# Hash attention and RWKV channel mix on one core: one PSUM pool, joined bucket bits, attention output turned by DMA, wanted times per pair

## Chip, core, metric

One core of a Trainium2 chip (trn2). The metric is the device time of one execution in microseconds (us), the median of several. The kernel before takes 258.7 us (258.31 to 258.94 in three runs; with a fourth, the median is 258.6).

Engine names: PE is the matmul engine and PEld its weight loads, DVE the vector engine, ACT the scalar engine, POOL the third elementwise engine, SP the engine that issues most DMAs.

## The reference, cut to what matters

Four batches of eight heads, 768 rows of 64 columns. Each row of q and k gets a bucket number from the signs of six projections; a query sees only keys of its own bucket. The eight heads of a batch, side by side, are x (768 x 512) of the channel mix.

```python
q_bits = (einsum('bhsd,dk->bhsk', q, proj) > 0)        # k_bits the same
mask   = q_bucket[..., :, None] == k_bucket[..., None, :]
scores = where(mask, q @ k.T / sqrt(64), -1e9)
attn   = exp(scores - max) / sum                       # then attn @ v
# x: the heads of a batch side by side; x_prev: x moved down by one row
xk = mu_k * x + (1 - mu_k) * x_prev                    # xr the same with mu_r
k  = maximum(xk @ w_k, 0)
out = sigmoid(xr @ w_r) * ((k * k) @ w_v)
```

## The kernel before

It works on 16 pairs of heads, four to a batch; the channel mix of a batch can run once its four pairs are done. The instruction order is made while the kernel is built: every operation is given to a small planner with a duration, an engine and a wanted time; the planner plays the whole kernel through and emits the operations in that order. The order is fixed on every engine. In the traces the instructions of PE, ACT and DVE, and the DMAs that SP issues, follow the order of the built program one for one; an engine whose next instruction has to wait stands still.

The planner also hands out PSUM. PSUM is the memory that matmuls write to. The kernel uses it as eight banks (512 columns of 32 bits in each of 128 partitions). Before, they are declared as two score tiles of two banks and four small tiles of one bank each:

```python
sc_t = [psum.tile([P, STEP], FP32, name=f"sc{i}", tag=f"sc{i}") for i in range(2)]   # STEP = 1024: two banks
sm_t = [psum.tile([P, 512], FP32, name=f"sm{i}", tag=f"sm{i}") for i in range(4)]    # one bank
plan = Plan({"sc": (2, 2), "sm": (4, 3)})
def sm(name):
    return sm_t[plan.slot[name]]
```

The softmax here doesn't subtract the row's maximum and nothing guards it: scores larger than these inputs give would overflow.

## Time and profile before

| | before |
|---|---|
| device time, median | 258.7 us |
| span of the profiled run | 256.8 us |
| PE / DVE / ACT / POOL busy | 239.3 / 195.1 / 185.5 / 57.9 us |
| ACT idle, waiting for scores | 28.3 us |
| first matmul of the first channel mix | us 63.4 |

The head of the page of the kernel before: the span, the busy time of each engine with its share and number of instructions, and PE's row of the 40 equal slices (a digit is tenths busy).

```profile
span 256.8 us, 6319 instructions
...
PE 239.3 (93%) x2519; PEld 143.5 (56%) x2519; DVE 195.1 (76%) x391; ACT 185.5 (72%) x242; POOL 57.9 (23%) x98
...
PE   6768898888999999999999989999999999999994
```

PE has holes only in the first quarter and is full after that.

The page's groups of one step of the mix, before. Columns: line, engine, operation, out<-in, count | busy us, mean ns of one | idle us of the engine just before, and what ended it.

```profile
L652 PE MATMUL sm<-xk,wk 128*128 128x384 bf16 x256 | 48.9, 326 | 0.2
...
L656 ACT ACTIVATE kr<-sm 128x384 bf16<-128x384 f32 x64 | 31.3, 498 | 9.5 <-PE sm L652 7.5
...
L659 DVE TENSOR_TENSOR k<-kr 128x384 bf16<-128x384 bf16 x64 | 23.8, 385 | 8.5 <-ACT kr L656 8.4
```

PE stood 0.2 us in all before these 256 matmuls.

At us 20, in the start, ACT stood 3.9 us for scores of pair 0 (ACT's timeline of the kernel before):

```profile
20.20 2.90 ACT L557 ACTIVATE pt<-sc 128x1024 bf16<-128x1024 f32 x3 [3.86 <-PE sc L553]
```

### The profile page before, as it was taken

The page shows a single profiled execution, that of the slowest core. Times are in us where ns is not written, and L with a number is a line of the kernel's source. Part 1 is how long each engine was busy: PE and PEld are TensorE (multiplying, and loading weights), DVE is VectorE, ACT ScalarE, POOL GpSimd, SP SyncE. Part 2 cuts the span into 40 slices and gives each one's busy share as a digit, 9 for nine tenths or more (in the row PEclk, how much of TensorE's full clock was granted, in tenths as well). Part 3 has the DMA queues.
Part 4 walks back from the last instruction along what each step waited for, and adds up shares of the span by engine and source line. Part 5 has one row for each costly group of instructions (what it writes and reads, how often), then busy time and mean ns, then how long its engine had stood idle before and what let it go on. Part 6 is the DMA issues. An engine that isn't in the chain of part 4 may idle for free.

```text
span 256.8 us, 6319 instructions
## 1 busy us (share of the span) xinstructions
PE 239.3 (93%) x2519; PEld 143.5 (56%) x2519; DVE 195.1 (76%) x391; ACT 185.5 (72%) x242; POOL 57.9 (23%) x98
## 2 busy tenths in 40 slices
PE   6768898888999999999999989999999999999994
PEld 2334564555666456656666655555666666555441
DVE  4999676777789997989998999898685753675322
ACT  3838888888994598878898967586798986147320
POOL 2491415056051330504041424040000000000000
PEclk9998999999999999999999999999999999999999
DMA  6968979799998479796978987888200011220132
GB/s 191 382 168 155 163 174 172 199 171 180 225 201 227 116 199 175 212 241 190 274 148 266 216 241 149 233 164 166 89 3 6 3 41 43 82 86 1 41 123 82
DMA packets 64565, 39.78 MB, mean 155 GB/s; under 512 B 46756, under 2 KB 60952, under 8 KB 64536
## 3 DMA queue, kind: packets, MB, share of 16 engines
q1 hardware_dynamic: 62248, 36.76, 58.4%
q0 software_dynamic: 2208, 2.62, 6.3%
q8 instruction: 19, 0.31, 0.5%
q14 instruction: 10, 0.08, 0.1%
q10 hardware_dynamic: 80, 0.00, 0.0%
HBM read 24.12 MB, written 6.29 MB: 118 GB/s over the span
## 4 chain that ended last, share of the span: by engine, by line
PE 63%; DMA 15%; DVE 10%; POOL 3%; SPq 3%; issue 2%; ACT 2%; POOLq 0%; DVEq 0%
PE sc L553 16%; PE sm L681 15%; PE sm L652 11%; PE sm L583 10%; DMA vn<-in_v_dram 8%; PE sm L671 7%; PE sm L443 4%; DMA qn<-in_q_dram 3%; DMA ak<-kh 2%; POOL vt L360 2%; DMA kn<-in_k_dram 2%; PE sm L609 2%; ACT pt L557 2%; SPq L334 1%; DVE xk L635 1%
## 5 line engine op out<-in xcount | busy, mean ns | idle before, releaser
L557 ACT ACTIVATE pt<-sc 128x1024 bf16<-128x1024 f32 x144 | 143.2, 1028 | 29.9 <-PE sc L553 28.3
L553 PE MATMUL sc<-aq,ak 128*128 128x512 f16 (+1 forms) x384 | 84.6, 329 | 4.5 <-ACT pt L557 4.5
L553 PEld LDWEIGHTS <-ak 128*128 128x128 f16 x384 | 33.6, 98 | 31.1 <-issue 12.2
L652 PE MATMUL sm<-xk,wk 128*128 128x384 bf16 x256 | 48.9, 326 | 0.2
L681 PE MATMUL sm<-wv,k 128*128 128x512 bf16 x192 | 47.8, 379 | 1.1 <-DVE ob L599 1.1
L583 PEld LDWEIGHTS <-pt 128*128 128x128 bf16 x1152 | 42.9, 97 | 9.0 <-issue 0.6
L583 PE MATMUL sm<-va,pt 128*128 128x65 bf16 x1152 | 44.6, 193 | 0.0
L656 ACT ACTIVATE kr<-sm 128x384 bf16<-128x384 f32 x64 | 31.3, 498 | 9.5 <-PE sm L652 7.5
L652 PEld LDWEIGHTS <-wk 128*128 128x128 bf16 x256 | 24.1, 98 | 15.2 <-issue 0.3
L360 POOL TENSOR_TENSOR vt<-vn 128x384 f32<-128x384 f32 x12 | 15.1, 1256 | 71.5 <-DMA vn<-in_v_dram 71.5
L659 DVE TENSOR_TENSOR k<-kr 128x384 bf16<-128x384 bf16 x64 | 23.8, 385 | 8.5 <-ACT kr L656 8.4
L674 ACT ACTIVATE rs<-sm 128x512 f32<-128x512 f32 x24 | 14.4, 599 | 22.1 <-PE sm L671 18.9
L681 PEld LDWEIGHTS <-k 128*128 128x128 bf16 x192 | 18.4, 98 | 19.5 <-issue 1.3
L688 DVE SCALAR_TENSOR_TENSOR os<-rs,sm 128x512 f32<-128x512 f32 x24 | 16.3, 684 | 16.5 <-PE sm L681 16.4
L671 PE MATMUL sm<-wr,xr 128*128 128x512 bf16 x96 | 24.6, 379 | 0.0
L619 POOL COPY xt<-xt 128x127 bf16<-128x127 bf16 x16 | 8.4, 525 | 69.1 <-DVE xt L615 64.4
L447 DVE TENSOR_SCALAR bx<-sm 128x384 uint16<-128x384 uint16 (+1 forms) x32 | 16.4, 549 | 3.3 <-PE sm L443 2.6
L599 DVE TENSOR_TENSOR ob<-sm,rc 128x384 bf16<-128x384 f32 x32 | 17.8, 556 | 0.9
L405 DVE SCALAR_TENSOR_TENSOR kh<-kn,kh 128x768 f16<-128x768 f32 x15 | 18.3, 1219 | 0.1
L635 DVE SCALAR_TENSOR_TENSOR xk<-df,muk,xt 128x768 bf16<-128x768 bf16 x16 | 16.7, 1046 | 0.3
L443 PE MATMUL sm<-ak,p 128*32 128x384 f16 x124 | 14.4, 335 | 2.3 <-DVE ak L422 1.3
L635 DVE SCALAR_TENSOR_TENSOR xr<-df,mur,xt 128x768 bf16<-128x768 bf16 x16 | 16.1, 1018 | 0.0
(76 smaller groups left out, 195.3 us busy)
## 6 DMA issues: line engine op xcount, KB each, us to landing
vn<-in_v_dram SPq DMA_DIRECT2D x16, 384.0 KB
out_dram<-os SPq DMA_DIRECT2D x24, 256.0 KB
qn<-in_q_dram SPq DMA_DIRECT2D x15, 384.0 KB
kn<-in_k_dram SPq DMA_DIRECT2D x15, 384.0 KB
wk<-in_moe_w_k_dram POOLq DMA_DIRECT2D x4, 256.0 KB, 5.3
wv<-in_moe_w_v_dram POOLq DMA_DIRECT2D x4, 256.0 KB, 8.7
wr<-in_moe_w_r_dram POOLq DMA_DIRECT2D x2, 256.0 KB, 5.4
aq<-bx SPq DMA_DIRECT2D x31, 9.0 KB
```

What stands on the lines that cost most here:

```text
L360: nc.gpsimd.tensor_tensor(out=vt[:, :, :, 0:E], in0=src[:, :, 0:3, 0:E], in1=src[:, :, 3:6, 0:E], op=ALU.add)
L405: nc.vector.scalar_tensor_tensor(out=nh[:, :, D:P], in0=nat.rearrange("p j (c d) -> p (j c) d", d=D), scalar=QS, in1=nh[:, :, 0:D], op0=AL ...
L443: nc.tensor.matmul(ps[32 * i : 32 * i + 32, 0:HALF], w_, a[:, i // 2, h * HALF : (h + 1) * HALF], start=st, stop=not st)
L553: nc.tensor.matmul(ps[:, lo - s * STEP : hi - s * STEP], side_a["k"][sa][:, j, jc * P : (jc + 1) * P], side_a["q"][sa][:, j, q0 : q0 + hi ...
L557: nc.scalar.activation(out=pt_t[sp][:, s * STEP : (s + 1) * STEP], in_=sc_t[plan.slot[nm]], func=AF.Exp, bias=EBIAS, scale=ESC)
L583: nc.tensor.matmul(oo[:, ic * 65 : ic * 65 + 65], pt_t[sp][:, o : o + P], va_t[sa][:, j, jc, 0 : D + 1], start=(not uc and ic == 0 and jc ...
L635: nc.vector.scalar_tensor_tensor(out=dst[smx], in0=df_t[sd], scalar=mu[:, t : t + 1], in1=x, op0=ALU.mult, op1=ALU.add)
L652: nc.tensor.matmul(ps[:, 0:HALF], wk_sb[:, d, fc * P : (fc + 1) * P], xk_t[mx[d]][:, h * HALF : (h + 1) * HALF], start=(d == 0), stop=(d = ...
L656: nc.scalar.activation(out=kr_t[sk], in_=sm(nm)[:, 0:HALF], func=AF.Relu, scale=0.5 ** 0.5)
L659: nc.vector.tensor_tensor(out=k2_t[s2][:, h * HALF : (h + 1) * HALF], in0=kr_t[sk], in1=kr_t[sk], op=ALU.mult)
L671: nc.tensor.matmul(sm(nr), xr_t[mx[d]][:, c * P : (c + 1) * P], wr_sb[:, d, :], start=(d == 0), stop=(d == NDC - 1))
L681: nc.tensor.matmul(sm(nv), k2_t[(b * NFC + fc) % NK2][:, c * P : (c + 1) * P], wv_sb[:, fc, :], start=(fc == 0), stop=(fc == NFC - 1))
```

## The change

The intent: use PSUM as one pool, so that a third score tile can exist when small tiles leave room; join the two bucket-bit tiles of a pair in one two-bank tile; let DMA transpose the attention output of 11 pairs (PE did it); take q and k of pair 2 to PE; issue bucket-row DMAs from ACT; split the fused mixes of xk and xr into two cheaper DVE instructions; and search wanted times afresh, with own values for the first six pairs. The core of the diff, cut:

```diff
-    NPET = 1
+    NPET = 2
+    ROW_ACT = (0, 1)
+    OT_PE = (0, 1, 2, 3, 15)
 ...
-    sc_t = [psum.tile([P, STEP], FP32, name=f"sc{i}", tag=f"sc{i}") for i in range(2)]
-    sm_t = [psum.tile([P, 512], FP32, name=f"sm{i}", tag=f"sm{i}") for i in range(4)]
-
-    plan = Plan({"sc": (2, 2), "sm": (4, 3)})
+    ps_t = [psum.tile([P, STEP], FP32, name=f"ps{i}", tag=f"ps{i}") for i in range(4)]
+
+    plan = Plan((0, 1, 2), (7, 6, 5, 4), {"sc": 3, "sm": 4}, 3)
     def sm(name):
-        return sm_t[plan.slot[name]]
+        b_ = plan.slot[name]
+        return ps_t[b_ // 2][:, (b_ % 2) * 512 : (b_ % 2) * 512 + 512]
 ...
+                (nc.scalar if on_act else nc.sync).dma_start(out=side_a[side][sa][D : D + NB, j, :], in_=bx_t[sx][...])
 ...
+            nc.sync.dma_start_transpose(out=xt_t[sx][:, P:].rearrange("p (c q) -> p c q", q=P),
+                                        in_=ob_t[so].rearrange("p c d -> p (c d)"))
 ...
+                nc.vector.tensor_scalar(out=tm_t[tm], in0=df_t[sd], scalar1=mu[:, t : t + 1], scalar2=mc[:, 0:1], op0=ALU.mult, op1=ALU.add)
+                nc.vector.tensor_tensor(out=dst[smx], in0=tm_t[tm], in1=x, op=ALU.add)
```

The eight banks are now four tiles of two banks, and a small tile is a half of one of them.

## The prediction

> **What bounds it now.** The busy table has PE at 93% (239.3 of 256.8 us), DVE 76%, ACT 72%. In dense stretches the timeline shows PE at its streaming rate: four 512-column matmuls in 0.86 us, twelve PV matmuls in 0.38 us. Counting all matmuls at such rates gives 228 us of PE work (my estimate), so about 29 us of the span is not PE work. In windows of 16 us, counted the same way, PE loses about 8, 6, 3 and 4 us in the first four (21 us before us 64), about 1 us in most later ones or less, and 4 us after the last matmul. From us 64, when the channel mix of batch 0 starts, only less PE work helps. Before that it is the start: loads, DVE (10.6 to 13.5 of 16 us busy) and ACT's exponentials (1.03 us each, nine per pair), which waited 28 us for scores in all, once 3.9 us at us 20.
>
> **What the change does.**
> - PE: the output transposes of 11 pairs (66 of 96) go to DMA; q and k of pair 2 come to PE (24). Net 42 fewer at about 58 ns: -2.4 us on the bound engine. The bucket matmuls stream the same columns.
> - DVE: 11 evictions of the attention output (about 600 ns) vanish; 32 bucket-bit evictions of 550 ns become 16 double ones, perhaps 0.95 us each; four copies of 0.55 us are added for pair 2. The 24 fused multiply-adds for xk and xr of pairs 4 to 15 (1018 to 1046 ns) become a tensor_scalar plus a tensor_tensor. The Trainium skill ("VectorE: DVE Perf Modes", Rules for kernel authors) gives dense 16-bit data 4x on copy/scalar and 2x on tensor_tensor; the trace agrees for the second (df, same size, 615 ns); I estimate 0.35 us for the first, so only -2 us. In all DVE loses 8 to 10 us, mostly where it is not the bound.
> - PSUM: three score tiles instead of two when the small tiles leave room. ACT waits less for scores; worth something only in the first 60 us. Later two or three small tiles remain for the channel mix: a risk of new PE waits.
> - DMA: 11 transposes more (half size), two fewer of full size; DMA is busiest at us 48 to 80 (share 1.04 and 1.15).
> - Bucket-row DMAs of pairs 0 and 1 issue from ACT: [...]eight of them.
> - Per-pair times reorder the start. PE's order shows the channel mix beginning after 123 score matmuls (120 before): no earlier in the work, so the start must get denser. ACT alone needs about 57 us to reach that point (10 us, then 46 exponentials), against 64 now: a ceiling near 7 us. I count 4 to 5 us.
>
> **Sum.** 258.7 - 2.4 (PE work) - 4.5 (start) - 1 (small waits) = 250.8. Predicted 250.5 us, 8 in 10 between 246.0 and 255.5. Faster by over 2%: 0.75; within 2%: 0.22; slower: 0.03.
>
> **What would show it.** PE busy falls by 2 to 4 us; its idle time before us 64 falls most; the channel mix starts at us 59 to 61 instead of 64.9; ACT waits for scores well below 28 us; PE full afterwards; DVE busy about 186 us; tail unchanged at 4 us.
>
> **What would make it wrong.** Output transposes by DMA landing late, so that xk and xr hold up the channel mix; PE waiting on PSUM evictions with fewer small tiles; DMA congestion delaying q/k loads; or the start held by DVE or loads as before, leaving only the 2.4 us. A start at ACT's own pace would make it better than 248.

## More of the kernel before

The planner only orders. The waits come from the framework that the kernel is written in, which sees each instruction's tiles. Part of the channel mix: four matmuls fill a small tile, ACT takes relu out of it, DVE squares.

```python
def f(nm=nm, fc=fc, h=h):                                                 # PE
    for d in range(NDC):
        nc.tensor.matmul(sm(nm)[:, 0:HALF], wk_sb[...], xk_t[...], start=(d == 0), stop=(d == NDC - 1))
def g(nm=nm, sk=sk):                                                      # ACT
    nc.scalar.activation(out=kr_t[sk], in_=sm(nm)[:, 0:HALF], func=AF.Relu, scale=0.5 ** 0.5)
def g2(sk=sk, s2=s2, h=h):                                                # DVE
    nc.vector.tensor_tensor(out=k2_t[s2][...], in0=kr_t[sk], in1=kr_t[sk], op=ALU.mult)
```

From pair 4 on, the column mean of v is taken out before the product with the attention weights: POOL sums v's rows (the tile vs), one PE matmul adds over partitions, DVE subtracts.

The timeline of the last batch shows how the three engines turn over (columns: start, length, engine, line, instruction, count, idle before and what ended it):

```profile
228.18 9.26 PE L652 MATMUL sm<-xk,wk 128*128 128x384 bf16 x56
...
229.03 0.49 ACT L656 ACTIVATE kr<-sm 128x384 bf16<-128x384 f32 x1 [1.02 <-PE sm L652]
...
229.55 0.36 DVE L659 TENSOR_TENSOR k<-kr 128x384 bf16<-128x384 bf16 x1 [0.48 <-ACT kr L656]
229.68 0.49 ACT L656 ACTIVATE kr<-sm 128x384 bf16<-128x384 f32 x1 [0.16 <-PE sm L652]
...
230.33 0.49 ACT L656 ACTIVATE kr<-sm 128x384 bf16<-128x384 f32 x1 [0.16 <-PE sm L652]
```

56 matmuls stand in one unbroken row of PE (9.26 us, 0.165 us each) while ACT takes one small tile every 0.65 us, which is just the time of the four matmuls of the next one.

## The result

| | before | after |
|---|---|---|
| device time, median | 258.6 us | 294.6 us (293.7 to 294.9) |
| ratio, 95% interval | | 1.137 (1.134 to 1.141) |
| span | 256.8 us | 293.1 us |
| PE / DVE / ACT busy | 239.3 / 195.1 / 185.5 us | 248.7 / 188.5 / 184.1 us |
| ACT idle, waiting for scores | 28.3 us | 29.8 us |
| first matmul of the first channel mix | us 63.4 | us 73.7 |

A ratio is the mean time of one kernel's fast runs over that of the other's fast runs of the same rounds, so it is not quite the ratio of the medians quoted. The change is slower by 14%. All four runs of the kernel before lie within 0.25%. The granted clock is no rival: 0.988 to 0.994 in the runs of the change, 0.986 to 1.0 in those of the kernel before that were taken with the experiments. (The prediction puts the start of the mix before at us 64.9; the first of its matmuls stands at us 63.4 in the trace.)

The head of the page, after:

```profile
span 293.1 us, 6295 instructions
...
PE 248.7 (85%) x2477; PEld 143.3 (49%) x2477; DVE 188.5 (64%) x392; ACT 184.1 (63%) x242; POOL 55.6 (19%) x110
...
PE   6846888779998789899979899988988999888974
```

PE has holes all the way through, and no other engine is near full: something makes the engines wait for each other. The same groups as before:

```profile
L720 PE MATMUL ps<-xk,wk 128*128 128x384 bf16 x256 | 48.1, 325 | 9.1 <-ACT kr L724 5.3
...
L724 ACT ACTIVATE kr<-ps 128x384 bf16<-128x384 f32 x64 | 29.2, 492 | 31.3 <-PE ps L720 19.7
L727 DVE TENSOR_TENSOR k<-kr 128x384 bf16<-128x384 bf16 x64 | 24.0, 381 | 24.3 <-ACT kr L724 23.9
```

The durations are those of before; the waits are not. ACT idles 31.3 us before its relus (9.5 before), DVE 24.3 us before its squares (8.5), and PE, which never stood here, 9.1 us. A timeline of the last batch, after, shows the shape of it:

```profile
258.17 1.46 PE L720 MATMUL ps<-xk,wk 128*128 128x384 bf16 x8 [0.60 <-ACT rs L742]
...
259.66 0.87 ACT L724 ACTIVATE kr<-ps 128x384 bf16<-128x384 f32 x2 [1.55 <-PE ps L720]
...
260.58 2.11 PE L720 MATMUL ps<-xk,wk 128*128 128x384 bf16 x12
...
262.08 1.25 ACT L724 ACTIVATE kr<-ps 128x384 bf16<-128x384 f32 x3 [1.55 <-PE ps L720]
...
263.00 2.11 PE L720 MATMUL ps<-xk,wk 128*128 128x384 bf16 x12 [0.31 <-ACT kr L724]
...
264.56 1.25 ACT L724 ACTIVATE kr<-ps 128x384 bf16<-128x384 f32 x3 [1.23 <-PE ps L720]
```

The eight matmuls at us 258.17 are two small tiles, banks 7 and 6, both halves of the tile ps3. The first four are finished after half of the 1.46 us, and in the kernel before ACT would take them then. Here ACT begins at us 259.66, at the end of all eight, and does both relus in a row. The next matmuls into ps3 wait until the relus are out: PE stood 0.31 us at us 263.00 for them. Producer and consumer alternate where they used to overlap.

To see how much PE got done, I counted the matmuls of each trace at the streaming rates of the prediction (a 512-column matmul 0.2165 us, a 384-column one 0.1625, a PV matmul 0.0315, a transpose 0.058). The sums are estimates; PE work finished by a given time, in us:

```
kernel             us 64   us 128   us 192   us 256   whole
before                42      105      168      231     231
after                 36       90      146      198     228
b1_joined             41       93      147      206     229
a1_split67            41       98      157      221     229
x2_vearly             42      101      163      226     227
z2_search             42      104      167      227     227
```

The changed kernel is 6 us behind after 64 us, and from there loses 7 to 11 more in each 64 us, to the end. (The other rows are the experiments below. Rows of like instructions are merged in the view, so the sums are good to about 2 us. A recount from every record of the packed traces, at about the same rates, gives 41, 103, 164 and 225 us before and 35, 89, 143 and 194 us after: the same gaps within 2 us.) The loss is not one accident but a lower pace.

The start has a loss of its own. ACT's timeline, after:

```profile
17.01 1.02 ACT L605 ACTIVATE pt<-ps 128x1024 bf16<-128x1024 f32 x1 [1.94 <-PE ps L601]
19.09 1.26 ACTq L507 DMA_DIRECT2D aq<-bx  x1
20.45 0.68 ACTq L507 DMA_DIRECT2D ak<-bx  x1
...
24.27 2.85 ACT L605 ACTIVATE pt<-ps 128x1024 bf16<-128x1024 f32 x3 [6.24 <-DMA ak<-bx]
```

ACT computes nothing for 6.2 us, which the trace puts down to a bucket row (3.9 us at this place before, put down to scores). From us 19.1 to 24.2 of that it issues six row DMAs itself, at 0.68 us each and 1.26 for the first, and its next exponential starts as soon as the last is issued. The granted clock from us 16 to 32 was 0.79 here and 0.89 before; no run tells what that cost.

Where the DVE estimates of the prediction landed, from the groups of the changed kernel:

```profile
L493 DVE TENSOR_SCALAR bx<-ps 128x768 uint16<-128x768 uint16 x15 | 14.2, 950 | 3.6 <-PE ps L490 3.5
...
L703 DVE TENSOR_TENSOR xk<-tm,xt 128x768 bf16<-128x768 f16 x12 | 6.7, 558 | 0.3
...
L700 DVE TENSOR_SCALAR tm<-df,mur,mc 128x768 f16<-128x768 bf16 x12 | 5.9, 492 | 0.2
```

The joined bucket eviction costs 0.95 us as estimated. The new tensor_scalar took 0.47 to 0.49 us against my 0.35, so tensor_scalar plus tensor_tensor (1.04 us) saves nothing over the fused instruction (1.02 to 1.05 us). DVE was busy 64% of the span; no run tests whether this mattered.

### The profile page after: what moved, and what is told of

Same layout as the page of the kernel before. It is cut to its first block, busy times and chain, and to the rows that moved or that the text cites. A ratio compares the mean times of both kernels' runs of the same rounds, so it can differ in the third digit from the quotient of the medians.

```text
span 293.1 us, 6295 instructions
## 1 busy us (share of the span) xinstructions
PE 248.7 (85%) x2477; PEld 143.3 (49%) x2477; DVE 188.5 (64%) x392; ACT 184.1 (63%) x242; POOL 55.6 (19%) x110
## 4 chain that ended last, share of the span: by engine, by line
PE 54%; DVE 20%; ACT 11%; issue 7%; DMA 6%; POOL 1%; SPq 1%; DVEq 0%; ACTq 0%; POOLq 0%
PE ps L749 12%; PE ps L720 11%; PE ps L631 11%; PE ps L601 9%; ACT kr L724 5%; PE ps L739 5%; ACT pt L605 3%; DMA vn<-in_v_dram 3%; DVE ob L647 3%; DMA qn<-in_q_dram 3%; DVE os L756 3%; DVE bx L493 3%; PE ps L490 2%; DVE qh L452 2%; ACT rs L742 2%
## 5 line engine op out<-in xcount | busy, mean ns | idle before, releaser
L605 ACT ACTIVATE pt<-ps 128x1024 bf16<-128x1024 f32 x144 | 140.3, 1032 | 36.1 <-PE ps L601 29.8
L601 PE MATMUL ps<-aq,ak 128*128 128x512 f16 (+1 forms) x384 | 81.7, 328 | 5.7 <-DMA ak<-bx 2.9
L720 PE MATMUL ps<-xk,wk 128*128 128x384 bf16 x256 | 48.1, 325 | 9.1 <-ACT kr L724 5.3
L749 PE MATMUL ps<-wv,k 128*128 128x512 bf16 x192 | 48.1, 378 | 6.4 <-ACT rs L742 2.9
L631 PE MATMUL ps<-va,pt 128*128 128x65 bf16 x1152 | 45.9, 194 | 7.8 <-DVE os L756 2.0
L724 ACT ACTIVATE kr<-ps 128x384 bf16<-128x384 f32 x64 | 29.2, 492 | 31.3 <-PE ps L720 19.7
L727 DVE TENSOR_TENSOR k<-kr 128x384 bf16<-128x384 bf16 x64 | 24.0, 381 | 24.3 <-ACT kr L724 23.9
L720 PEld LDWEIGHTS <-wk 128*128 128x128 bf16 x256 | 24.3, 97 | 29.4 <-issue 14.8
L756 DVE SCALAR_TENSOR_TENSOR os<-rs,ps 128x512 f32<-128x512 f32 x24 | 16.4, 684 | 22.1 <-PE ps L739 10.7
L739 PE MATMUL ps<-wr,xr 128*128 128x512 bf16 x96 | 24.6, 379 | 0.5 <-DVE rc L642 0.3
L647 DVE TENSOR_TENSOR ob<-ps,rc 128x384 bf16<-128x384 f32 x32 | 17.8, 555 | 7.5 <-PE ps L720 2.3
L452 DVE SCALAR_TENSOR_TENSOR qh<-qn,qh 128x768 f16<-128x768 f32 x15 | 15.4, 1028 | 0.1
```

What stands on the lines that cost most here:

```text
L452: nc.vector.scalar_tensor_tensor(out=nh[:, :, D:P], in0=nat.rearrange("p j (c d) -> p (j c) d", d=D), scalar=QS, in1=nh[:, :, 0:D], op0=AL ...
L601: nc.tensor.matmul(ps[:, lo - s * STEP : hi - s * STEP], side_a["k"][sa][:, j, jc * P : (jc + 1) * P], side_a["q"][sa][:, j, q0 : q0 + hi ...
L605: nc.scalar.activation(out=pt_t[sp][:, s * STEP : (s + 1) * STEP], in_=ps_t[plan.slot[nm]], func=AF.Exp, bias=EBIAS, scale=ESC)
L631: nc.tensor.matmul(oo[:, ic * 65 : ic * 65 + 65], pt_t[sp][:, o : o + P], va_t[sa][:, j, jc, 0 : D + 1], start=(not uc and ic == 0 and jc ...
L647: nc.vector.tensor_tensor(out=ob_t[so][:, :, j * D : (j + 1) * D], in0=oo[:, :, 0:D], in1=rc_t[sr][:, 1, :].unsqueeze(2).to_broadcast([P, ...
L720: nc.tensor.matmul(ps[:, 0:HALF], wk_sb[:, d, fc * P : (fc + 1) * P], xk_t[mx[d]][:, h * HALF : (h + 1) * HALF], start=(d == 0), stop=(d = ...
```

## The experiments

**Theory A**: the framework keeps its waits per tile, so two banks in one tile make false waits: a reader of one bank waits for the writer of the other, and the reverse. **Rival B**: the new order, the outputs turned by DMA, or the rows on ACT cost the time. Theory A allows a check without a chip. In the built programs I compared each wait with the last instruction that really touched the same bank (an eviction is an ACT or DVE instruction that reads a result out of PSUM; a PE instruction also waits for its SBUF operands, which this count cannot set apart, so its column does not go to zero):

```
program          evictions that wait for PE work beyond     PE instructions on PSUM that wait for
                 their own bank, of those that wait         ACT or DVE beyond their own bank
before                     0 of 344                                   8 of 294
after                     90 of 289                                  87 of 264
b1_joined                 75 of 307                                 124 of 269
a1_split67                 8 of 324                                  15 of 276
z2_search                  0 of 329                                  13 of 284
```

Of the 90 evictions after, 89 wait for exactly the last matmul into the other bank of their tile, and so do all 75 of b1_joined. That shows that the false waits exist; what they cost needed runs. Replanning is a trap here: any change of a duration or a pool makes the planner emit another order. So several kernels keep the order of every engine and change one thing. Whether an order is identical was checked instruction by instruction.

### b1_joined: the kernel before, its small tiles joined two by two

```diff
-    sm_t = [psum.tile([P, 512], FP32, name=f"sm{i}", tag=f"sm{i}") for i in range(4)]
+    sm_t = [psum.tile([P, 1024], FP32, name=f"sm{i}", tag=f"sm{i}") for i in range(2)]
-        return sm_t[plan.slot[name]]
+        s_ = plan.slot[name]
+        return sm_t[s_ // 2][:, (s_ % 2) * 512 : (s_ % 2) * 512 + 512]
```

> The kernel before with its four one-bank PSUM tiles declared as two tiles of two banks; every engine's instruction order is identical, only the waits differ (in the built program 75 of 307 evictions now wait for matmuls beyond their own bank, 0 before). Theory A (waits are kept per tile, so two banks in one tile make false waits, and that is the bulk of the +36 us): clearly slower than before, 275 to 295 us. Rival B (the loss comes from the new instruction order, the DMA-turned outputs or the bucket rows on ACT): 257 to 262 us.

Measured 285.2 us against 260.0 of the kernel before on the same chip, ratio 1.096 (1.091 to 1.102). The head of its page:

```profile
span 283.5 us, 6326 instructions
...
PE 245.7 (87%) x2519; PEld 143.6 (51%) x2519; DVE 196.2 (69%) x391; ACT 187.5 (66%) x242; POOL 52.8 (19%) x98
...
PE   6767988897959998988999899778998999999994
```

The same 2519 matmuls in the same order, and PE's full rows are gone. Declaring two one-bank tiles as one costs 25 us in a kernel that is otherwise untouched. This is theory A alone; B, which expected 257 to 262 us, has nothing to say about it.

### a1_split67: the changed kernel, banks 6 and 7 apart again

```diff
-    ps_t = [psum.tile([P, STEP], FP32, ...) for i in range(4)]
+    ps_t = [psum.tile([P, STEP], FP32, ...) for i in range(3)]
+    pb_t = {i: psum.tile([P, 512], FP32, name=f"pb{i}", tag=f"pb{i}") for i in (6, 7)}
     def sm(name):
         b_ = plan.slot[name]
+        if b_ >= 6:
+            return pb_t[b_]
```

> The changed kernel with banks 6 and 7 as two tiles of their own instead of one of two banks; instruction order on every engine identical to the changed kernel. Theory A: most of the loss goes, 258 to 268 us; what stays above 251 is the start (ACT held 5 us by the bucket-row DMAs) and the shared banks 4 and 5. Rival B: 288 to 295 us, as the order is the same.

Measured 270.3 us, ratio 1.041 (1.034 to 1.049), where the changed kernel has 1.137. The two ratios are 0.096 apart, which is 25 us of 259: two thirds of the loss (24.3 us in medians), with the order of the changed kernel unaltered. (Its near twin a0_f6, below, ran at 292.8 us, 22.5 us above a1_split67.) It stays 2 us above the range that I gave, and 4% slower than the kernel before, so something else is left: up to a third of the loss may be B's. In its timeline the relus start tile by tile again:

```profile
242.59 0.81 PE L723 MATMUL ps<-xk,wk 128*128 128x384 bf16 x4
...
243.24 1.46 PE L723 MATMUL pb<-xk,wk 128*128 128x384 bf16 x8
...
243.44 0.49 ACT L727 ACTIVATE kr<-ps 128x384 bf16<-128x384 f32 x1 [0.16 <-PE ps L723]
...
244.09 0.49 ACT L727 ACTIVATE kr<-pb 128x384 bf16<-128x384 f32 x1 [0.16 <-PE pb L723]
```

### a2_sep and a0_f6: the old division replanned, and its control

a2_sep gives the changed kernel two score tiles and four one-bank tiles. a0_f6 is the changed kernel with one mended dependency, which a2_sep needs too: the planner gave back the mean's PSUM tile after an instruction that could be planned before two other readers of the tile. In replanned variants this really happens: a2_sep without the mended dependency is stopped by the simulation ahead of the chip, for reading a bank in the middle of an accumulation. In the changed kernel itself the order happens to be right.

```diff
-        add("DVE", DVE_C(1), R("va", n), f6, r=[(nm,)], w=[("mc", sm_)], give=[nm])
+        add("DVE", DVE_C(1), R("va", n), f6, r=[(nm,), ("va", sa, 0), ("va", sa, 1)], w=[("mc", sm_)], give=[nm])
```

> The changed kernel with the score tiles (two) and four one-bank tiles apart again, as in the kernel before, the plan made anew, everything else of the change kept (with a mended order of the last reader of the mean tile). Theory A: 252 to 264 us. Rival B: above 280 us, as the DMA-turned outputs, the rows on ACT and the wanted times are kept.

> Control: the changed kernel with only the mended dependency (the column mean is computed after the two centred halves of v, so the tile is given back after its last reader), which moves a few instructions. Both theories: 290 to 300 us, within 2% of the changed kernel; if it is far from that, the time hangs on small order changes.

a0_f6 measured 292.8 us (1.126), as expected. a2_sep measured 281.6 us (1.082), against both: its small tiles are apart, and it is not below 264. By itself this looks like support for B. But the end time that the planner itself arrives at, which is its opinion and no measurement, is 271 us for a2_sep and 243 us for the changed kernel (249 for the kernel before): wanted times that were searched for one pool make a poor plan for another. The last two kernels below, which keep most of B's suspects (not the rows on ACT) and have wanted times searched for the new pool, say more. a2_sep as an experiment was confounded by its plan and carries no weight for either theory.

### What is left in a1_split67

In a1_split67 PE's longest waits are two: 4.1 us for a bucket row in the start, and the mean's matmul. PE's waits (engine, line, waited for: us, times, longest):

```profile
PE pb L429 <- POOL vs L416: 5.5, 5, 2.3
PE ps L604 <- DMA ak<-bx: 4.1, 1, 4.1
PE ps L429 <- POOL vs L416: 2.4, 1, 2.4
```

The chain of waits leads from the mean's matmul to the load of v, and that to the SP queue. SP's timeline at that place:

```profile
81.86 0.74 SPq L510 DMA_DIRECT2D aq<-bx  x1
...
84.67 0.44 SPq L384 DMA_DIRECT2D kn<-in_k_dram  x1
85.21 0.71 SPq L510 DMA_DIRECT2D ak<-bx  x1
86.02 0.39 SPq L389 DMA_DIRECT2D vn<-in_v_dram  x1
```

and the chain from there:

```profile
86.02 4.34 DMA vn<-in_v_dram
...
90.49 1.73 POOL vt L410
...
92.79 1.01 POOL vs L416
...
93.85 0.22 PE pb L429
```

v is issued behind four bucket rows on the SP queue, which issues in the planned order, lands 4.3 us later, POOL sums it, and PE stands 1.8 us at the mean's matmul. Four kernels, each a1_split67 with one edit, were run on one chip.

**x1_rowsp**: rows of pairs 0 and 1 from SP.

```diff
-                (nc.scalar if on_act else nc.sync).dma_start(out=...)
+                nc.sync.dma_start(out=...)
```

> On a1_split67 (270.3 us): the six bucket-row DMAs of pairs 0 and 1 issue from SP instead of ACT, everything else in the same order. If the rows on ACT cost the start (ACT issued them from us 19 to 24 and the next exponential came 6.2 us after the last), 3 to 6 us come back: 264 to 267. If the start is bound by the rows' own landing, as in the kernel before, no change (269 to 271), or worse, as SP is the busier queue.

**x2_vearly**: the loads of v earlier on SP.

```diff
     order = plan.schedule()
+    for n in range(6, NPAIRS):
+        i = next(i for i, o in enumerate(order) if o.name == f"ldv{n}")
+        o, passed = order.pop(i), 0
+        while i and passed < 10 and order[i - 1].i not in o.deps:
+            i -= 1
+            passed += order[i].eng == "SP"
+        order.insert(i, o)
```

> On a1_split67: the loads of v for pairs 6 to 15 are issued up to ten places earlier on SP, all other engines in the same order. Theory C (v lands late behind bucket rows and output transposes on the in-order SP queue, and PE then stands at the mean's matmul: 7.9 us of PE waits for the sum of v plus 9.5 us of weight-load idle there): 262 to 266 us, and the waits of the mean's matmul go below 2 us. Rival (the waits only move to the next late operand): 268 to 271.

**x3_plain**: plain copies in place of the transposes of the attention output.

```diff
-            nc.sync.dma_start_transpose(out=xt_t[sx][:, P:].rearrange(...), in_=ob_t[so].rearrange(...))
+            nc.sync.dma_start(out=xt_t[sx][:, P:], in_=ob_t[so].rearrange("p c d -> p (c d)"))
```

> On a1_split67: the 11 transposing DMAs of the attention output become plain copies of the same bytes (wrong result on purpose), same order. Theory D (the transposes themselves, by their time on DMA and on the SP queue, cause the remaining loss): 260 to 264 us. If they only arrive late because of what stands before them, 268 to 271.

**x4_xslate**: POOL's shift of the transposed output moved to just before its first user.

```diff
     order = plan.schedule()
+    for n in range(NUC, NPAIRS):
+        if n not in OT_PE:
+            o = order.pop(next(i for i, o in enumerate(order) if o.name == f"xs{n}"))
+            order.insert(next(i for i, p in enumerate(order) if p.name == f"df{n}"), o)
```

> On a1_split67: on POOL, the copy that shifts the DMA-turned output stands just before its first user instead of right after the transpose was planned, so POOL does not stand waiting for the transpose (67 us of POOL waits) with sums of v behind it. If this in-order wait is what delays the sums of v: 262 to 267 us. If the sums wait for v's load anyway: 269 to 271.

| | median us of the fast runs | ratio, 95% interval |
|---|---|---|
| a1_split67 (other chip) | 270.3 | 1.041 (1.034 to 1.049) |
| x4_xslate | 269.7 | 1.045 (1.033 to 1.055) |
| x1_rowsp | 268.0 | 1.038 (1.030 to 1.046) |
| x3_plain (wrong result, meant) | 266.4 | 1.029 (1.021 to 1.038) |
| x2_vearly | 265.6 | 1.024 (1.015 to 1.033) |

(One run of the kernel before and one of x4_xslate were slow; ratios use the fast ones.) x4_xslate changes nothing: POOL's 67 us of waiting for transposed outputs is idle time that costs nothing here, although it tops the list of waits. x2_vearly gains 4 to 5 us over x4_xslate on the same chip (4.1 us in medians, 0.02 in ratios, with intervals that just don't touch), as theory C expected, and the waits of the mean's matmul for the sum of v are gone. Its own list of PE waits:

```profile
PE ps L604 <- DMA ak<-bx: 4.2, 1, 4.2
PE ps L604 <- DVE bx L496: 2.3, 4, 1.7
PE pb L429 <- DVE ob L650: 1.8, 1, 1.8
```

x1_rowsp missed its 264 to 267: about 2 us, and the interval overlaps that of a1_split67, so a gain from the rows is not shown, though ACT's wait at that place fell from 6.0 to 4.5 us in the profiles. x3_plain missed its 260 to 264: 3 to 4 us under x4_xslate, with intervals that overlap, and less than the 6 to 10 that I gave the transposes.

### y1_rowsp_vearly and y2_all: sums of these

y1 is x1 and x2 together, y2 adds x3.

```diff
 y1:  edits of x1_rowsp and x2_vearly on a1_split67
 y2:  edits of x1_rowsp, x2_vearly and x3_plain on a1_split67 (wrong result, meant)
```

> a1_split67 with both x1 (rows on SP) and x2 (v loads earlier). If the two losses are separate, their gains add: about 2 + 4.5 us off 270, that is 262 to 265 us. If they share one queue and one delay, no better than x2 alone (265 to 267).

> y1 with the output transposes also turned into plain copies (wrong result on purpose), same order. If the transposes cost time by themselves once v is not behind them: 258 to 261 us. If their only cost was to delay v on the SP queue: as y1 within 1 us.

y1 measured 263.8 us (median of its three fast runs), 1.020 (1.006 to 1.034): inside its range, but the rows add nothing clear to x2. y2 measured 261.5 us, 1.009 (1.003 to 1.015), just above its 258 to 261, so the transposes as transposes may cost about 1% (1.020 to 1.009) once v is out of their way; the intervals overlap, so this is not shown.

### z1_search and z2_search: the change with tiles apart and a plan made for it

All of the change, with a pool in which no two small tiles share a tile: banks 6 and 7 on their own, bank 5 or the third score pair but not both. Rows on SP. The planner's costs raised to what the traces show (2.1 us of SP for a q or k transpose, 0.78 for a row, 1.35 for an output transpose, landing 0.6 us later, and no DMA of SP or ACT issued before the eighth one before it has landed, as the waits in the built program have it), and wanted times searched for the planner's end time. z1 and z2 are two results of that search.

```diff
-    plan = Plan((0, 1, 2), (7, 6, 5, 4), {"sc": 3, "sm": 4}, 3)
+    plan = Plan((0, 1, 2), (7, 6, 5), {"sc": 3, "sm": 3}, 3)
-    ROW_ACT = (0, 1)
+    ROW_ACT = ()
+    (banks 6 and 7 as in a1_split67; the dependency of a0_f6; other PR and PX; the planner's costs)
```

> A version to beat both: all of the change, but no two small tiles share a PSUM tile (banks 6 and 7 own tiles, bank 5 or the third score pair), rows on SP, the planner given SP and landing times as the traces show them, and wanted times searched anew for that. If the false waits and the plan's missing SP time were the causes, 248 to 256 us; if something else in the change is slow, above 262.

> As z1, another result of the same search. 248 to 256 us, within 3 us of z1, if the planner's times are now near the truth; above 262 if something else in the change is slow.

z1 measured 258.4 us, 0.999 (0.992 to 1.005), z2 258.0 us, 0.997 (0.991 to 1.002), both correct. The head of z2's page and its longest PE wait:

```profile
span 255.5 us, 6302 instructions
...
PE 238.5 (93%) x2477; PEld 143.7 (56%) x2477; DVE 189.4 (74%) x392; ACT 184.9 (72%) x242; POOL 55.6 (22%) x110
```

```profile
PE pb L608 <- DVE qh L593: 5.0, 2, 4.6
```

They miss the 248 to 256 that I gave, and do not clearly beat the kernel before: the intervals hold 1. But they keep the outputs turned by DMA (plain copies in their place were not tried here), the joined bucket bits, pair 2 on PE and a third score tile, and run 36 us faster than the changed kernel. Rival B in the form "these parts are slow" falls, except for the rows on ACT, which z1 and z2 leave out (x1_rowsp found no clear gain from that). Why the 2.4 us saved on PE (estimated) do not show in the time was not tested. In z2's start PE stands 4.6 us at the transposes of q of pair 2, which the change brought into PE's list, while DVE prepares q; and from us 16 to 32 PE was busy 11.0 us at a granted clock of 0.79, against 13.1 us at 0.89 before.

## Why the prediction was wrong

The prediction was 250.5 us (246.0 to 255.5), faster with 0.75; the result is 294.6.

1. **The step that failed** is the PSUM point, "three score tiles instead of two when the small tiles leave room ... Later two or three small tiles remain for the channel mix: a risk of new PE waits", and with it "PE full afterwards". I counted tiles and gave the waits a gain of 1 us ("- 1 (small waits)"). The number of tiles was not the matter; that two banks were one tile was. In place of -1 the runs showed about +25 us: a1_split67 takes that off the changed kernel, with its order kept. b1_joined puts 25 us on the kernel before, again with its order kept; it joins other banks, so that the two sizes agree is chance, but both have the one cause. The risk named, too few small tiles, was not this one: in z2_search no two small tiles share a tile, at most three exist at a time, and the loss is gone.
2. **The start** ("I count 4 to 5 us") did not come. The mix began at us 73.7, not at 59 to 61. With tiles apart (a1_split67) PE work done by us 64 is 41 us against 42 before, so the new wanted times made the start no denser; the false waits then cost 5 us more of it.
3. **A term was missing**: the in-order SP queue. The prediction counted DMA's share of time, and named "DMA congestion delaying q/k loads" and late outputs. It was v, issued behind rows, that held PE: 4 to 5 us (x2_vearly against x4_xslate). The output transposes may cost about 1% (y2_all against y1_rowsp_vearly, not clear of noise). "Output transposes by DMA landing late, so that xk and xr hold up the channel mix" is not what the traces show: in the changed kernel and in a1_split67 no wait of PE is for xk or xr, and moving the POOL copy that waits for the transposes changed nothing (x4_xslate).
4. **Right**: 42 matmul instructions fewer (2519 to 2477), 2.4 us by estimate; DVE busy 188.5 us (about 186 predicted); the joined eviction 0.95 us; the tail unchanged. PE busy did not fall, it rose to 248.7 us. Each burst shows about 0.16 us beyond its matmuls (4 in 0.81 us, 8 in 1.46, 12 in 2.11, 56 in 9.26), and the change has more bursts without a gap between matmuls (92, against 30 before and 24 in z2_search); with the tiles apart (z2_search) PE busy is 238.5. The tensor_scalar was mis-sized (0.35 for 0.48 us); its effect on the time was not tested.
5. **Open**: of the roughly 270 - 258 = 12 us between a1_split67 and z2_search, 4 to 5 us are the loads of v; the rest came with the new plan and was not divided further. The cost of banks 4 and 5, which a1_split67 still shares with a score tile, was not measured. Whether a longer search of the kernel before would gain as well was not tried.

The Trainium skill, "PSUM — Partial Sum Buffer", section "PSUM bank collisions raise a hardware error", asks to guard PSUM by bank and quadrant, "by bank is the simple version". The kernel before did that, since each small tile was a bank. After, the guard was by two banks, coarser than the rule asks; b1_joined prices the difference at 25 us of 260. (No run here provokes a collision.)

## What to carry to other kernels

Make the unit on which waits are kept (here the declared tile) no larger than the unit that you hand out; when a pool is merged, compare what each wait really waits for in the built programs before and after, since names and counts of tiles don't show it. A plan searched with a model is only good for the resources that the model knows: here it knew banks but not tiles, and took SP's issues for cheaper than they were. Nor need such a plan survive a change of pool (a2_sep, 281.6 us); here a new search was needed. To test a part of such a change, keep the emitted order and change one thing; a replanned variant tests its plan.

## What the Trainium skill lacked or had wrong

- No page says that waits kept per declared tile make false waits between banks of one tile. Measured: 25 us of 260 (b1_joined). It belongs to "PSUM — Partial Sum Buffer".
- "VectorE: DVE Perf Modes", Rules for kernel authors, says of elementwise work on matmul output to "accept 1× (PSUM src)". Here a copy of 768 16-bit columns out of PSUM took 548 ns, as long as the tensor_tensor on SBUF that the page gives 2x (558 ns); the fused instruction on SBUF took 1018 to 1046. For 32-bit sums the rule fits (384 columns in 555 ns). The page's own tier table (at most 2x for PSUM) agrees with the trace, its rule does not.
- The same page gives dense 16-bit tensor_scalar 4x. With two per-partition scalars, bf16 to fp16, 768 columns took 472 to 492 ns, 10 to 15% under the 2x tensor_tensor (546 to 558 ns); if it ran at 4x, little of that reached the duration.
- The same page, "The three transpose paths", gives 390 ns for a 128x128 transpose on PE. In the kernel before six of them end 0.51 us after the first starts. Issued in a row, the rate matters, not the single latency.
- "DMA: Bandwidth & Descriptors", Rules for kernel authors, says that spreading DMAs over engines "only saves sequencer issue time". Here that time is large: 0.68 us for a 9 KB row DMA, on ACT and on SP alike, and 1.22 to 1.89 us of SP for an output transpose. The page gives issue costs only in its part on trn3, in cycles and for earlier generations; none for trn2 and DMAs like these.
